# Seven half-size output products in the form with shared sums, one core of a Trainium2 chip

## The chip, the cores and the metric

The kernel runs on one core of a Trainium2 chip. A core has a matrix engine (TensorE, PE in the profile, with its weight loads listed apart as PEld), a vector engine (VectorE, DVE), a scalar engine (ScalarE, ACT), a general engine (GpSimd, POOL) and a queue engine that issues most transfers (SyncE, SP). Matmul results go to PSUM, which has eight banks of 512 fp32 columns by 128 partitions here. Each engine takes its instructions in order and waits on semaphores for the others. The metric is the device time of the program in microseconds (us); lower is better.

## What is computed

Linear attention without a mask over 8 batches, 8 heads, 576 positions and head size 64, followed by a two-layer network with an exact gelu. Cut to what matters:

```python
def _attn_ref(q, k, v):                      # 8 x 8 x 576 x 64
    q_s = softmax(q, axis=-1)
    k_s = softmax(k, axis=2)
    kv = np.einsum('bhsd,bhse->bhde', k_s, v)
    return np.einsum('bhsd,bhde->bhse', q_s, kv)

def _moe_ref(x, w_in, w_out):                # x: 4608 x 512
    h = x @ w_in                             # 512 x 2048
    g = 0.5 * h * (1.0 + erf(h / sqrt(2)))
    return g @ w_out                         # 2048 x 512
```

The attention's output, with heads side by side, is `x`; the output is 4608 x 512 in fp32. The tolerance lets the matmuls run in bf16.

## The kernel before

**Chunks.** The 4608 rows are worked in nine chunks of 512 rows (`M`): chunk c = 0 to 7 takes the first 512 rows of batch c, and chunk 8 the last 64 rows (`R`) of all eight batches. For a chunk: exp of q and k on ACT (`exp_q`, `exp_k`), the sums of q and its scaling (`q_sums`, `q_scale`), a transpose of q by DMA (`xbar_step`), the matmuls of k and v (`kv_step`), the attention's output `xT` (`x_all`), the first layer with gelu into `g` (2048 x 512, bf16), and the second layer into the output. The attention for the next chunks is put between the matmuls of the second layer. The order within every engine is the order in which the program is written (`manual_schedule`), so the text of the kernel is the order of all queues.

**First layer.** Chunks 0 and 1 use plain matmuls (`h_phase`, `h_pairs`). From chunk 2 on `h_waves` uses a scheme with seven products of half-size blocks instead of eight, in a form where products add up in PSUM: letters A, B, C name the banks in which they do, and `r` a copy in SBUF. Its last lines turn the last two groups of A and of B into `g` by gelu, then make sums of blocks of `g` on DVE (`s_parts`). `turn_roles` then renames the PSUM banks for the next chunk; the names `bb`, `ba`, `x0` to `x3`, `kv0`, `kv1` stand for the eight banks.

**Second layer.** `g` is cut into four blocks, halves of the 2048 features (`UP`, `DN`) by halves of the 512 rows (`LO`, `HI`); `w_out` likewise into four, features by halves of the 512 columns. Chunk 0 uses plain matmuls (`y_mm`); chunks 1 to 7 use `y_phase` and chunk 8 `y_last`. These use seven products of half-size blocks too. The operands of a product are listed in `y_operands`; sums of blocks of `w_out` are made once by `mix_wo` into `w16` and `w7` or in place, and sums of blocks of `g` by `s_parts` for each chunk into `s12`, `s5` or in place. A product is 16 matmuls of 256 columns (two groups of 128 rows by eight groups of features; 8 in `y_last`, which treats the two groups of rows after each other).

In `y_phase` before, five banks (`bd`, `be`, `bb`, `bx`, `ba`) take the products. The common part, product 4 minus product 5, is kept in SBUF in fp32 (`f`, which is the tile `zeros32`); ACT or DVE copies or adds each product into the output tiles `y_sb`, and POOL adds two of the four blocks to the block `c22` (L848 to L851). Two products add up in one bank only where a bank is begun anew. `f` is copied by DVE in chunk 1 (L823) and by ACT from chunk 2 on (L814).

In chunks 3 to 7 product 3 is itself computed by a seven-product scheme with quarter-size blocks (`class Two`): 28 matmuls of 128 columns (L753) in place of 16 of 256. For it POOL makes five sums of weights once (`weights`), DVE makes three kinds of sums of `g` for each half of the features in each chunk (`sums`: `rows`, `diag`, `cols`), ACT copies a snapshot of the partial result (`snap`, `two_d`), and POOL corrects it (`corner`, `corner2`) and adds it to two blocks (`spread`).

**Work between the products.** `y_phase` gets a dictionary of functions and calls `after(i)` behind named points; the loop at the end of the kernel fills it: exp of q and k two chunks ahead on ACT, sums of q on DVE, casts of v and scaling of q on POOL, the load of a later chunk on SP, and before the last product `next_x` (the next chunk's x, the transpose, k and v matmuls). In front of `y_phase(1)` the program issues `exp_q(2, parts=2)` and `exp_k(2)`.

## Time and profile before

| | |
|---|---|
| median of 3 runs | 255.81 us (255.73 to 255.81) |
| span of the profiled execution, first to last instruction | 253.9 us |
| granted TensorE clock | 0.997 |
| chunk 1's products begin (chain) | 58.5 us |
| chunk 2's products begin | 85.3 us |
| chunks 3 to 7: products begin | 111.1, 136.8, 162.4, 188.0, 213.0 us |
| chunk 8's products begin | 238.1 us |
| PE's last matmul ends | 250.3 us |
| DVE busy from 124.5 to 150.1 us (one chunk) | 24.4 of 25.6 us |
| DVE busy from 238.1 to 250.3 us | 9.1 of 12.2 us |

The median is the whole device time of the program; the span is that of one execution taken with the profiler, and 1.9 us of the median lie outside it. Line numbers (L799) are those of the kernel before. A line can be that of a helper: all additions made by `tt` have L444, so these are told apart by their tiles (`y_sb`, `two`, `two_d`, `r`, `qb`). PE's matmuls are pipelined: the timeline gives the time of issue and a modelled end, the chain the stretch for which a group holds the chain, which begins 0.17 us later.

### The profile page before, as it was taken

How to read it: one execution, taken by the hardware profiler on the slowest of the kernel's cores; microseconds unless marked ns; L12 is line 12 of the kernel's file. 1: busy time of each engine (PE TensorE's matmuls, PEld its weight loads, DVE VectorE, ACT ScalarE, POOL GpSimd, SP SyncE). 2: the span in 40 equal slices, each digit the busy share in tenths (PEclk: the TensorE clock that was granted, in tenths of full speed). 3: DMA queues.
4: the chain of work that ended last, by engine and by line, in shares of the span. 5: the costliest groups of instructions: out<-in, count | busy, mean ns of one | idle time of the engine just before them, and what ended most of it. 6: DMA issues, size and time to landing. Idle time of an engine off the chain costs nothing.

```text
span 253.9 us, 6825 instructions
## 1 busy us (share of the span) xinstructions
PE 247.9 (98%) x2738; PEld 196.1 (77%) x2738; DVE 219.1 (86%) x395; ACT 190.4 (75%) x326; POOL 102.8 (40%) x177
## 2 busy tenths in 40 slices
PE   7999999999999999999999999999999999999994
PEld 3444444448888888898889988998889889988883
DVE  1878898788987997998999899989999999868972
ACT  4785978699977996889688968896887788248711
POOL 1530023000978459106950596059603960560000
PEclk9999999999999999999999999999999999999998
DMA  7999999995329999890569255810520061004033
GB/s 239 397 367 420 405 406 400 401 407 206 61 64 288 375 265 377 246 340 5 188 196 310 98 188 177 204 36 3 165 87 3 1 193 57 3 4 165 0 84 84
DMA packets 43168, 50.24 MB, mean 198 GB/s; under 512 B 20225, under 2 KB 30465, under 8 KB 42881
## 3 DMA queue, kind: packets, MB, share of 16 engines
q1 hardware_dynamic: 42416, 49.13, 57.8%
q10 hardware_dynamic: 720, 0.69, 1.0%
q8 instruction: 21, 0.34, 0.6%
q14 instruction: 11, 0.08, 0.1%
HBM read 36.70 MB, written 9.44 MB: 182 GB/s over the span
## 4 chain that ended last, share of the span: by engine, by line
PE 81%; DMA 16%; DVE 1%; SPq 0%; issue 0%
PE qa L513 19%; PE ya L799 10%; PE qb L513 10%; PE yd L799 10%; DMA f<-in_q_dram 7%; PE ye L799 6%; PE ps L393 6%; PE yb L799 5%; PE qc L513 5%; DMA w<-in_moe_w_out_dram 3%; DMA w<-in_moe_w_in_dram 3%; PE yx L753 3%; DMA f<-in_v_dram 2%; PE kv L231 2%; PE ps L359 1%; PE ya L882 1%
## 5 line engine op out<-in xcount | busy, mean ns | idle before, releaser
L513 PEld LDWEIGHTS <-quad_s 128*128 128x128 bf16 x448 | 43.8, 98 | 5.1
L799 PEld LDWEIGHTS <-g 128*128 128x128 bf16 x368 | 35.2, 98 | 4.8 <-issue 0.4
L513 PEld LDWEIGHTS <-wi_bf 128*128 128x128 bf16 x336 | 32.8, 98 | 3.9
L799 PEld LDWEIGHTS <-s 128*128 128x128 bf16 x336 | 32.7, 98 | 3.7
L513 PE MATMUL qa<-quad_t,quad_s 128*128 128x256 bf16 x224 | 29.2, 273 | 0.0
L275 POOL TENSOR_TENSOR e<-e,recq 128x1024 bf16<-128x1024 bf16 (+1 forms) x4 | 9.3, 2330 | 47.8 <-DVE recq L270 41.0
L393 PE MATMUL ps<-xT,wi_bf 128*128 128x512 bf16 x128 | 28.1, 379 | 0.2 <-DVE kvc L244 0.2
L444 POOL TENSOR_TENSOR y_sb<-y_sb 128x128 f32<-128x128 f32 x56 | 26.0, 498 | 2.8 <-issue 2.8
L269 DVE TENSOR_REDUCE qsum<-e 128x16 f32<-128x1024 bf16 (+1 forms) x12 | 20.9, 1746 | 6.8 <-ACT e L179 6.5
L284 POOL TENSOR_TENSOR e<-e,recq 128x256 bf16<-128x256 bf16 x40 | 24.7, 653 | 1.8 <-DVE recq L270 1.2
L393 PEld LDWEIGHTS <-wi_bf 128*128 128x128 bf16 x128 | 12.4, 98 | 15.3 <-issue 0.7
L521 ACT COPY qc<-qa 128x512 f32<-128x512 f32 x26 | 13.9, 577 | 11.4 <-PE qa L513 5.3
L399 ACT ACTIVATE g<-ps 128x512 bf16<-128x512 f32 x32 | 17.6, 602 | 6.1 <-PE ps L393 5.8
L179 ACT ACTIVATE e<-f 128x512 bf16<-128x512 f32 (+1 forms) x42 | 20.5, 556 | 2.1 <-DMA f<-in_q_dram 1.9
L537 ACT ACTIVATE g<-r 128x512 bf16<-128x512 f32 x28 | 17.3, 631 | 6.3 <-DVE r L444 6.3
L444 DVE TENSOR_TENSOR qb<-qa,r 128x512 f32<-128x512 f32 x28 | 18.1, 691 | 4.1 <-PE qa L513 1.6
L537 ACT ACTIVATE g<-qc 128x512 bf16<-128x512 f32 x28 | 15.2, 594 | 7.4 <-PE qc L513 7.4
L418 DVE TENSOR_TENSOR s<-g 128x1024 bf16<-128x1024 bf16 x28 | 19.8, 726 | 0.0
L196 POOL CAST v_aug<-f 128x576 bf16<-128x576 f32 x25 | 17.0, 711 | 4.4 <-DMA f<-in_v_dram 4.3
L444 DVE TENSOR_TENSOR r<-qa,r 128x512 f32<-128x512 f32 x28 | 17.9, 680 | 0.7 <-PE qa L513 0.7
L184 ACT ACTIVATE ek<-f 128x2304 bf16<-128x2304 f32 (+1 forms) x10 | 17.2, 1734 | 1.2 <-DMA f<-in_k_dram 1.2
L1213 POOL CAST scr<-g 128x1 f32<-128x1 bf16 x4 | 0.7, 187 | 42.3 <-DVE g L421 42.3
(117 smaller groups left out, 550.2 us busy)
## 6 DMA issues: line engine op xcount, KB each, us to landing
out_dram<-y_sb SPq DMA_DIRECT2D x16, 512.0 KB, 3.9
f<-in_k_dram SPq DMA_DIRECT2D x6, 1152.0 KB, 9.5
f<-in_v_dram SPq DMA_DIRECT2D x6, 1152.0 KB, 10.5
f<-in_q_dram SPq DMA_DIRECT2D x6, 1024.0 KB, 7.6
w<-in_moe_w_in_dram SPq DMA_DIRECT2D x6, 512.0 KB, 8.9
f<-in_v_dram SPq DMA_DIRECT2D x8, 288.0 KB, 6.5
f<-in_q_dram SPq DMA_DIRECT2D x4, 512.0 KB, 9.0
w<-in_moe_w_out_dram SPq DMA_DIRECT2D x2, 1024.0 KB, 11.4
```

What stands on the lines that cost most here:

```text
L179: nc.scalar.activation(out=dst[:, i], in_=src[:, u], func=AF.Exp)
L184: nc.scalar.activation(out=ek[b % 2][:, i:i + n], in_=st[b]["kf"][:, i:i + n].rearrange("p x (n d) -> p x n d", n=NS), func=AF.Exp,)
L196: eng.tensor_copy(out=o, in_=i)
L269: nc.vector.reduce_sum(out=qsum, in_=st[b]["eq"][:, :, i * w:(i + 1) * w, :], axis=AX.X)
L284: nc.gpsimd.tensor_tensor(out=e, in0=e, op=ALU.mult, in1=st[b]["recq"][:, j, i:i + 4].unsqueeze(2).to_broadcast([128, 4, D]),)
L393: nc.tensor.matmul(ps, wi_bf[:, dm, t * 128:(t + 1) * 128], st[c]["xT"][:, dm, :], start=(dm == 0), stop=(dm == NDM - 1),)
L399: nc.scalar.activation(out=st[c]["g"][:, t, :], in_=ps, func=AF.Gelu)
L418: tt(out=s12[:, a, half], in0=g[:, a, half], in1=g[:, b, hi], op=ALU.add)
L444: eng.tensor_tensor(out=out, in0=in0, in1=in1, op=op)
L513: nc.tensor.matmul(held[kind, q][:, u], w, mov[m][:, k], start=(m in (1, 5) and u == 0 and k == 0), stop=(k == 1), skip_group_check=True,)
L537: nc.scalar.activation(out=g[:, t:t + 2, half], in_=held[kind, q], func=AF.Gelu)
L799: nc.tensor.matmul(ps[:, j * HN:(j + 1) * HN], act[m][:, k, j * 128:(j + 1) * 128], wgt[m][:, k, :], start=(first and k == 0 and j == 0), ...
```

## The change

The seven products of the second layer take another form of the scheme. With g's blocks a11 (`UP`, `LO`), a12 (`DN`, `LO`), a21 (`UP`, `HI`), a22 (`DN`, `HI`) and w_out's blocks b11, b12, b21, b22 there are four sums of each, each built on the one before:

- s1 = a21 + a22, s2 = s1 - a11, s3 = a11 - a21 (in place of a21), s4 = a12 - s2
- t3 = b22 - b12, t2 = t3 + b11, t4 = b21 - t2, t1 = b12 - b11 (in place of b12)
- products: 1: a11 b11, 2: a12 b21, 3: s4 b22, 4: a22 t4, 5: s1 t1, 6: s2 t2, 7: s3 t3

Product 1 is copied out by ACT (the first part of c11); products 6, 7 and 4 then add up on it in the same bank `pa`. Product 5 is copied out by DVE (into c22); after product 6 DVE writes pa + c22 into product 5's bank `pb`, and product 3 adds up there, which gives c12. Product 2 has a bank of its own, `pc`, and is added to c11 by DVE. After product 7 DVE adds pa to c22. After product 4 ACT copies pa out as c21. POOL does no addition of the output any more. The class `Two` and all that serves it are gone, for all chunks. `h_waves` puts gelu of the last two groups of B ahead of those of A, and the calls of `s_parts` are placed anew. The points of `after` and the functions at them change with the products.

```diff
     def s_parts(c, p0, n, which):
...
+        a11, a12, a21, a22 = g[:, a, lo], g[:, b, lo], g[:, a, hi], g[:, b, hi]
+        s1, s2, s4 = s5[:, a], s12[:, a, lo], s12[:, a, hi]
+        ops = {
+            1: (s1, a21, a22, ALU.add), 2: (s2, s1, a11, ALU.subtract),
+            3: (a21, a11, a21, ALU.subtract), 4: (s4, a12, s2, ALU.subtract),
+        }
+        for i in which:
+            tt(*ops[i])
...
+        gelu("B", 2, 3)
         gelu("A", 2, 3)
-        gelu("B", 2, 3)
-        if sums:
-            sums(c, 1)
-        else:
-            s_parts(c, 0, 4, (0,))
-            if mid:
-                s_parts(c, 0, 4, (4,))
-            s_parts(c, 0, 4, (2,))
-            s_parts(c, 4, 4, (0,))
-        s_parts(c, 4, 4, (3,))
-        s_parts(c, 4, 4, (4,))
+        s_parts(c, 0, 4, (2, 3, 4) if mid else (3, 4))
+        s_parts(c, 4, 4, (1, 2, 3, 4))
         turn_roles()
...
         wgt = {
+            1: wo_bf[:, UP, 0:HN], 2: wo_bf[:, DN, 0:HN], 3: wo_bf[:, DN, HN:DM],
+            4: w7, 5: wo_bf[:, UP, HN:DM], 6: w16[:, 1], 7: w16[:, 0],
         }
...
-    class Two:
...
+    def y_phase(c, ins):
...
+        at = {"ya": 2, "yb": 0, "yc": 3} if c == 1 else {"ya": roles["ba"], "yb": roles["bb"], "yc": roles["x0"]}
+        pa, pb, pc = (bank(at[n], n) for n in ("ya", "yb", "yc"))
...
+        mm(1, pa, True)
+        nc.scalar.copy(out=c11, in_=two(pa))
+        after(1)
+        mm(5, pb, True)
+        nc.vector.tensor_copy(out=c22, in_=two(pb))
+        after(5)
+        mm(6, pa, False)
+        tt(two(pb), two(pa), c22)
         after(6)
+        mm(2, pc, True)
+        tt(c11, c11, two(pc))
+        after(2)
+        mm(7, pa, False)
+        tt(c22, two(pa), c22)
         after(7)
+        mm(3, pb, False)
+        nc.scalar.copy(out=c12, in_=two(pb))
+        y_store(c, 0, ysb[0])
         after(3)
+        mm(4, pa, False)
+        nc.scalar.copy(out=c21, in_=two(pa))
         y_store(c, 1, ysb[1])
         after(4)
...
     def y_last(c):
...
+        sets = (("ba", "bb", "x0"), ("x2", "x1", "x3"))
...
         for j in range(2):
+            mm(j, 1, pa, True)
+            nc.scalar.copy(out=c11, in_=pa)
...
+            mm(j, 5, pb, True)
+            nc.scalar.copy(out=c22, in_=pb)
+            mm(j, 6, pa, False)
+            tt(pb, pa, c22)
+            mm(j, 2, pc, True)
+            tt(c11, c11, pc)
...
     y_phase(1, {
+        1: [sums[3], lambda: norm_q(2, 0, 2)],
+        5: [lambda: norm_q(2, 1, 2, nc.vector)],
+        6: [lambda: cast_v_all(3), lambda: xbar_step(2), lambda: exp_q(3)],
+        2: [lambda: kv_step(2), lambda: exp_k(3), lambda: q_sums(3)],
+        3: [lambda: table(AF.Gelu)],
         4: [lambda: load(4), lambda: x_all(2, (3, 4, 1, 5)),
...
     for c in range(2, B + 1):
...
         if nb <= B:
+            yi[1] = [lambda: exp_q(nb)]
+            yi[6] = [lambda: q_sums(nb), lambda: q_scale_parts(nb)]
+            yi[7] = [lambda: table(AF.Gelu)]
         if nb + 1 < B:
+            yi[6].append(lambda: load(nb + 1))
...
         if nb < B:
+            yi[5] = [lambda: exp_k(nb), touch_s, lambda: cast_v_all(nb)]
         if c < B:
+            yi[3] = [lambda: next_x(c, nb)]
+            y_phase(c, yi)
```

`touch_s` is a one-column copy on POOL from the last sum s4, which holds POOL's casts back until the sums are made; before, `touch_g` did so from `g`. `y_last` handles each of its two row groups in the same order of products; in the second one product 4 is made in two halves of 128 columns in two banks of their own, as product 7 was before.

## The prediction

> **What bounds the kernel now.** I read the page's shares first, then the chain of waits, then the timelines of ScalarE (ACT), VectorE (DVE) and TensorE (PE) around each place where the output products begin. From the page:

> ```profile
> PE 247.9 (98%) x2738; PEld 196.1 (77%) x2738; DVE 219.1 (86%) x395; ACT 190.4 (75%) x326; POOL 102.8 (40%) x177
> ...
> PE 81%; DMA 16%; DVE 1%; SPq 0%; issue 0%
> ```

> The chain is DMA until 41 us and then PE alone. It shows how evenly (start, length, what):

> ```profile
> 58.54 1.75 PE yd L799 x16
> 60.28 1.75 PE ye L799 x16
> ...
> 111.11 0.67 PE yx L753 x12
> ...
> 113.53 0.92 PE yx L753 x16
> ```

> From 44 to 250.3 us PE never pauses: each half-size product is 16 matmuls of 256 columns in 1.75 us (109 ns each), and the next begins where it ends. So an edit matters in two ways only: it changes what PE issues, or it makes PE wait. Work taken from DVE or POOL is worth nothing as long as PE does not wait for them now, and it does not.

> **The change, term by term.** All sums are in the profiled execution: span 253.9 us. The median of the runs is 255.81, so 1.9 us lie around the span, and I carry these over.

> *1. The inner scheme of product 3 (chunks 3 to 7).* Out go 12 + 16 matmuls of 128 columns, in come 16 of 256. The chain gives the 28 matmuls as 0.67 + 0.92 in three chunks and 0.67 + 0.97 in two, together 8.05 us; five times 1.75 is 8.75. PE: **+0.7** (bounds 0.55, all at 1.64, to 0.8, all at 1.59).

> *2. DVE and POOL.* Per chunk 3 to 7 DVE loses six small sums (0.41, 0.28, 0.41, twice: 2.2 us), two of ten wide sums (0.68 each) and one of five output operations (0.65): about 4.2 us. POOL loses the 56 adds of y_sb (26.0 us), the 30 on two_d and y_sb (16.1) and the weight sums (7.1). DVE's setup of w_out goes from ten operations of 0.69 to eight; DVE there waits 1.0 us for the load of w_out at 40.36, which hides either number. Each is **0**, since PE, which runs without a gap over all of them, is the cover; were it gone, DVE's 4.2 us a chunk would count.

> *3. New waits.* Before, five banks took the products and PE waited for no reader. Now products 6, 7 and 4 accumulate in the bank of product 1 and product 3 in that of product 5, so PE must wait until ACT has copied product 1 (before product 6), until DVE has read the bank after product 6 (before 7), and after 7 (before 4). The forms are all in the trace: ACT copies of 512 columns 0.57, DVE copies or adds from PSUM 0.63 to 0.69, also with PSUM as the output. I follow the waits chunk by chunk.

> *Chunk 1.* The copy of product 1 is on ACT; the first product's copy was on DVE (L823). ACT executes in order, and ahead of that copy it has exp of q and of k for chunk 2:

> ```profile
> 57.90 1.27 ACT L399 ACTIVATE g<-ps 128x512 bf16<-128x512 f32 x2
> 59.19 1.28 ACT L179 ACT_TABLE_LOAD   x1
> 60.48 2.38 ACT L179 ACTIVATE e<-f 128x512 bf16<-128x512 f32 x6
> 62.76 2.11 ACT L184 ACTIVATE ek<-f 128x2304 bf16<-128x2304 f32 x1
> 64.78 2.17 ACT L179 ACTIVATE e<-f 128x512 bf16<-128x512 f32 x4
> ```

> The copy takes the slot at 64.78, ends at 65.35, and product 6 can start at about 65.4. By PE's issue times, 0.17 ahead of the chain's, it was due at 61.87. PE waits **3.55 us**. Queued behind that copy on ACT are exp of q and k for chunk 3, each 0.5 us later, which DVE's sums of q need.

> Then PE: product 6 from 65.4, product 2 from 67.2, the k·v matmuls of chunk 2 at 69.0, product 7 at 69.8, product 3 at 71.5, product 4 due at 73.3. Behind the k·v matmuls DVE has four small operations (66.99 to 67.80 in the timeline), and then:

> ```profile
> 67.80 2.27 DVE L269 TENSOR_REDUCE qsum<-e 128x32 f32<-128x2048 bf16 x1
> 70.18 0.35 DVE L270 RECIPROCAL recq<-qsum 128x32 f32<-128x32 f32 x1
> 70.45 0.63 DVE L444 TENSOR_TENSOR y_sb<-y_sb,yb 128x512 f32<-128x512 f32 x1
> ```

> From k·v's end (69.9): 0.81 to the reduction, then 2.65 to the next add, now the one that reads the bank after product 7: 73.35 to 74.03. Product 4 starts at 74.1: **0.8 us** more. Chunk 1 costs 3.55 + 0.8 = **+4.35** (bounds 3.5, if the second wait is covered, to 4.6, with 0.2 for restarts; the trace's restart of PE behind DVE's kvc at 44.12 has 0.17 idle).

> *Chunk 2.* Product 5 is now second and needs sum 1 of all of g. DVE's second half of it stands fifth behind the r sums: from 84.36, the first taking 0.86, then 0.61 each, it runs 87.05 to 87.73. PE needs it at the fifth matmul of product 5, 85.14 + 1.75 + 0.44 = 87.33. With 0.1 for restart, 0.5; if the first takes 0.60, because POOL's tensor_scalar at its side (84.14 to 85.63) is gone, 0.25. I take **+0.4** (bounds 0 to 0.8).

> *Chunks 3 to 7.* In chunk 3, PE's last matmul of the first layer is issued at 110.95. ACT swaps its last two pairs of gelu, so those of half A run 111.88 to 112.96; the first frees product 5's bank at 112.5, due 112.70. Sum 1's second half starts at 112.03, when the B pair ends (DVE starts a wide sum there today, for the same reason), ends 112.71, needed 113.14. ACT's copy of product 1 ends 113.5, due 114.45. DVE after product 6: 116.4 to 117.1, due 117.94. The sums of q (2.65 us) hold the later adds to 119.75 to 120.95; the bank of product 2 is due at 121.4 for the next x, product 4 later still. All are covered, by 0.2 to 1 us: **0** (bounds 0 to 0.3 a chunk, 1.5 in all).

> *Last rows.* There a product lasts only 0.87 us, so the same gelu order is not covered (ACT, then PE):

> ```profile
> 236.76 1.23 ACT L537 ACTIVATE g<-r 128x512 bf16<-128x512 f32 x2 [0.56 <-DVE r L444]
> 237.89 1.07 ACT L537 ACTIVATE g<-qa 128x512 bf16<-128x512 f32 x2
> 238.85 1.09 ACT L537 ACTIVATE g<-qb 128x512 bf16<-128x512 f32 x2
> ```

> ```profile
> 237.91 1.04 PE L882 MATMUL yd<-wo_bf,g 128*128 128x256 bf16 x8
> 238.79 1.04 PE L882 MATMUL yx<-wo_bf,g 128*128 128x256 bf16 x8
> ```

> Product 5 is due at 238.79 and its bank is freed by the first gelu of the last pair, 239.45: **+0.7** (0.3 to 1.0). Later waits there fit by 0.1 to 0.2. The tail, two half products with an add and a store each, stays.

> *4. Queues.* SP's order becomes load, store, transpose, store; the transpose waits for POOL's scaling of q, until about 13.7 us after the products begin, and the store behind it frees a buffer that the next chunk needs 15 us later: **0**; without that cover a late store would delay ACT's or DVE's copy. The v load waits for POOL's casts, now done at about 6 us after the start instead of 10: **0**.

> **Sum:** 0.7 + 4.35 + 0.4 + 0 + 0.7 = 6.15 us; 255.81 + 6.15 = **262.0 us**.

> **Rivals.**
> *A. PE restarts slowly after chunk 1's pause.* At the kernel's start the weight loads show a slow phase:

> ```profile
> 5.87 0.34 PEld L1014 LDWEIGHTS ps<-zeros 128*128 128x128 f32 x1 [0.52 <-issue]
> 6.72 0.20 PEld L1014 LDWEIGHTS ps<-zeros 128*128 128x128 f32 x1 [0.52 <-issue]
> 7.16 0.19 PEld L1014 LDWEIGHTS ps<-zeros 128*128 128x128 f32 x1 [0.24 <-issue]
> ```

> Their spacing is 0.86 us until 6.72 and 0.43 after: half rate from 1.43 to 6.72, 5.3 us. If a 3.5 us pause brought that back, the same 5.3 us would hold 2.65 us less work: 264.65. Against it: no later pause in the trace is long enough to show it. [...]

> *B. The thin covers of chunks 3 to 7 fail too.* At 0.3 us each, +1.5: 263.5. For it: the cover of product 5's bank is 0.2 us; against: the timelines of those chunks repeat within 0.1 us.

> *C. Chunk 1's copy is covered.* That needs ACT to be free near 60.3, with exp of k done. Then 255.81 + 0.7 + 0.4 + 0.7 = 257.6. ACT's order is in the program, so little speaks for it.

> *D. Faster.* One mechanism: DVE and POOL traffic slows every matmul, and their relief lets it run. Place: the 1,560 full-size matmuls of chunks 2 to 8. Price: down to the weight load's mean of 98 ns, 11 ns each, -17 us: 245. It decides from 6.15 us / 1,560 = 4 ns each, below 105 ns. Against it: a matmul takes 109 ns in the last 12 us, where POOL is idle and DVE 74% busy, and also where DVE is 95% busy.

> **Chances.** Forecast 0.68, A 0.12, B 0.10, C 0.06, D 0.04. Adding the low bounds: 0.55 + 3.5 + 0 + 0.3 = 4.35, 260.2; the high ones without B: 0.8 + 4.6 + 0.8 + 1.0 = 7.2, 263.0. With A and B the range is 260.2 to 264.6. A measurement tells 0.2% (0.5 us) from no change; faster has D, 0.03, no change 0.01, slower 0.96.

> **What would show it.** A PE gap of 3.5 us at about 62 us, ended by ACT's copy of ya; a second, 0.8 us, before product 4, ended by DVE; 0.4 us within chunk 2's product 5; none of over 0.1 in chunks 3 to 7; 0.7 at the second product of the last rows; product 3 at 1.75 us everywhere. The prediction is wrong if ACT's copy comes before the exps, if PE's matmuls behind the first gap are not 109 ns apart, or if chunks 3 to 7 get longer by more than the 0.14 us of term 1.

## The result, and the profile after

| | before | after |
|---|---|---|
| median of the runs beside each other | 255.77 us (255.61 to 255.81) | 264.49 us (264.43 to 264.65, 4 runs) |
| ratio, 95% interval | | 1.0347 (1.0332 to 1.0361) |
| span of the profiled execution | 253.9 us | 262.4 us |
| granted TensorE clock in the mean | 0.997 | 0.993 |
| chunk 1's products begin (PE's issue) | 58.37 us | 58.10 us |
| chunk 2's first layer begins (PE's issue) | 72.81 us | 78.50 us |
| chunks 3 to 7: products begin (chain) | 111.1 to 213.0 us | 117.7 to 220.1 us |

The change makes the kernel slower by 8.7 us, where 6.15 were forecast. The page of the changed kernel, its shares and the chain's:

```profile
PE 251.1 (96%) x2678; PEld 196.9 (75%) x2678; DVE 190.0 (72%) x336; ACT 190.1 (72%) x324; POOL 54.5 (21%) x85
...
PEclk9999999999799999999999999999999999999999
...
PE 73%; DMA 12%; ACT 7%; DVE 4%; issue 1%; POOL 1%; ACTq 1%; SPq 0%; DVEq 0%
```

DVE gave up 29 us and POOL 48, and neither gave the program anything. ACT and DVE now hold 11% of the chain, where PE and DMA held 97% of it and DVE 1%. One slice of the clock row shows a 7: it covers 65.6 to 72.2 us. There stands chunk 1, here in PE's timeline of the changed kernel (time of issue, length, what; in brackets the idle time before and what ended it):

```profile
58.10 2.01 PE L684 MATMUL ya<-wo_bf,g 128*128 128x256 bf16 x16
59.95 1.91 PE L684 MATMUL yb<-wo_bf,s 128*128 128x256 bf16 x16
65.12 3.50 PE L684 MATMUL ya<-w,s 128*128 128x256 bf16 x16 [3.26 <-ACT y_sb L695]
68.41 2.03 PE L684 MATMUL yc<-wo_bf,g 128*128 128x256 bf16 x16
...
75.39 1.91 PE L684 MATMUL ya<-w,g 128*128 128x256 bf16 x16 [0.59 <-DVE y_sb L430]
```

Product 6 was due at 61.70 (59.95 + 1.75) and is issued at 65.12; then its 16 matmuls take 3.50 us where a product elsewhere shows 1.91. From issue to issue that is 3.29 us, 206 ns a matmul. The engines that PE waits for, in their timelines of the changed kernel, first ACT, then DVE:

```profile
60.21 2.37 ACT L173 ACTIVATE e<-f 128x512 bf16<-128x512 f32 x6
62.49 2.11 ACT L178 ACTIVATE ek<-f 128x2304 bf16<-128x2304 f32 x1
64.50 0.56 ACT L695 COPY y_sb<-ya 128x512 f32<-128x512 f32 x1
```

```profile
72.06 2.27 DVE L263 TENSOR_REDUCE qsum<-e 128x32 f32<-128x2048 bf16 x1
74.44 0.35 DVE L264 RECIPROCAL recq<-qsum 128x32 f32<-128x32 f32 x1
74.71 0.63 DVE L430 TENSOR_TENSOR y_sb<-ya,y_sb 128x512 f32<-128x512 f32 x1
```

The copy of product 1 stands behind exp of q and k, and the add after product 7 behind the sums of q, both as forecast. All waits of PE for another engine (total, times, longest, in us); those for `scr` and `kvc` lie in the kernel's opening, as in the kernel before, where they have 1.4 and 0.3 too:

```profile
PE ya L684 <- ACT y_sb L695: 3.3, 1, 3.3
PE ps L862 <- DVE scr L90: 1.4, 1, 1.4
PE ya L684 <- ACT g L522: 0.8, 1, 0.8
PE ya L684 <- DVE y_sb L430: 0.6, 1, 0.6
PE yb L737 <- ACT g L522: 0.6, 1, 0.6
PE ps L353 <- DVE kvc L238: 0.3, 1, 0.3
```

The third is in chunk 2, the fifth in the last rows. Their timeline lines, PE and the gelu ahead of it on ACT, then PE in the last rows:

```profile
90.62 1.07 ACT L522 ACTIVATE g<-qb 128x512 bf16<-128x512 f32 x2
91.58 1.09 ACT L522 ACTIVATE g<-qa 128x512 bf16<-128x512 f32 x2
```

```profile
91.74 1.91 PE L684 MATMUL ya<-wo_bf,g 128*128 128x256 bf16 x16 [0.83 <-ACT g L522]
...
246.79 1.03 PE L737 MATMUL yb<-wo_bf,s 128*128 128x256 bf16 x8 [0.55 <-ACT g L522]
```

Where the span's +8.5 us stand, each from the two timelines or chains: start of chunk 1's products -0.27 (why was not followed); pause before product 6 +3.42; half clock in products 6 and 2 +1.66 (3.29 us from issue to issue against 1.75, and 1.96 against 1.84); product 4's wait +0.75; chunk 2 +0.9; chunks 3 to 7 +0.7; last rows +0.7; from PE's last matmul to the end +0.5. The terms add up to 8.4; the rest is 0.1 in chunk 1's first product. Another 0.2 us of the median lie outside the span.

### The profile page after: what moved, and what is told of

Same layout as the page of the kernel before. It is cut to its first block, busy times and chain, and to the rows that moved or that the text cites. A ratio compares the mean times of both kernels' runs of the same rounds, so it can differ in the third digit from the quotient of the medians.

```text
span 262.4 us, 6525 instructions
## 1 busy us (share of the span) xinstructions
PE 251.1 (96%) x2678; PEld 196.9 (75%) x2678; DVE 190.0 (72%) x336; ACT 190.1 (72%) x324; POOL 54.5 (21%) x85
## 4 chain that ended last, share of the span: by engine, by line
PE 73%; DMA 12%; ACT 7%; DVE 4%; issue 1%; POOL 1%; ACTq 1%; SPq 0%; DVEq 0%
PE ya L684 18%; PE qa L498 16%; PE yb L684 8%; PE qb L498 8%; DMA w<-in_moe_w_in_dram 6%; PE ps L387 5%; PE yc L684 5%; PE qc L498 4%; DMA f<-in_v_dram 4%; ACT g L522 3%; PE ya L737 2%; DMA touch<-in_moe_w_out_dram 2%; PE kv L225 2%; PE ps L353 2%; PE yb L737 1%
## 5 line engine op out<-in xcount | busy, mean ns | idle before, releaser
L684 PEld LDWEIGHTS <-g 128*128 128x128 bf16 x448 | 43.3, 98 | 7.9 <-issue 2.2
L684 PEld LDWEIGHTS <-s 128*128 128x128 bf16 x336 | 33.6, 100 | 7.9 <-issue 3.4
L684 PE MATMUL ya<-w,g 128*128 128x256 bf16 x224 | 26.8, 273 | 0.6 <-DVE y_sb L430 0.6
L684 PE MATMUL yb<-wo_bf,s 128*128 128x256 bf16 x224 | 26.7, 273 | 0.0
L710 ACT COPY y_sb<-yb 128x512 f32<-128x512 f32 x7 | 4.1, 587 | 21.4 <-PE yb L684 21.4
L269 POOL TENSOR_TENSOR e<-e,recq 128x1024 bf16<-128x1024 bf16 (+1 forms) x4 | 9.3, 2332 | 48.8 <-DVE recq L264 48.8
L378 DVE CAST xT<-ps 128x512 bf16<-128x512 f32 x18 | 11.7, 687 | 10.0 <-PE ps L353 8.4
L684 PE MATMUL ya<-w,s 128*128 128x256 bf16 x112 | 15.0, 292 | 3.3 <-ACT y_sb L695 3.3
```

The costliest lines, as they stand in the source:

```text
L269: eng.tensor_tensor(out=e, in0=e, in1=st[b]["recq"].unsqueeze(3).to_broadcast([128, J, w, D]), op=ALU.mult,)
L378: nc.vector.tensor_copy(out=st[b]["xT"][:, hp, :], in_=ps)
L684: nc.tensor.matmul(ps[:, j * HN:(j + 1) * HN], act[m][:, k, j * 128:(j + 1) * 128], wgt[m][:, k, :], start=(first and k == 0 and j == 0), ...
```

## The experiments

Three questions were open: what the half clock costs and what brings it on (it was a rival of 0.12 and came in all four runs), whether the other terms are what the timelines say, and whether the new form is worth anything once its waits are gone.

### The clock behind the pause: filling it

In the first three kernels PE multiplies into an unused bank ahead of product 6 in chunk 1, 30, 12 and 4 times; the result is not used.

```diff
         after(5)
+        if c == 1:
+            fill = bank(4, "fill")
+            for i in range(30):
+                nc.tensor.matmul(fill[:, 0:HN], act[1][:, i % HK, 0:128], wgt[1][:, i % HK, :],
+                                 start=True, stop=True, skip_group_check=True)
         mm(6, pa, False)
```

> Thirty extra matmuls of 256 columns into a spare bank (109 ns each, 3.3 us) fill chunk 1's pause before product 6; nothing waits for them. If PE's idleness is what makes product 6 slow (3.50 us for 16 matmuls, granted clock 0.52), product 6 takes 1.75 us again, the pause itself stays in the form of extra matmuls, and the time is 264.5 - 1.7 = 262.8 us. If product 6 is slow for another reason (its operands, its bank, POOL or DVE at its side), it stays at 3.5 us and the time at 264.5.

Measured: 262.63 us (262.42 to 262.93), ratio 1.0275 (1.026 to 1.0291), granted clock 1.0 in every run. In PE's timeline of this kernel product 6 is back at its length, though it starts as long behind its due time as before (64.87 against 61.45, 3.42 us):

```profile
61.45 3.44 PE L703 MATMUL fill<-wo_bf,g 128*128 128x256 bf16 x30
64.87 1.91 PE L684 MATMUL ya<-w,s 128*128 128x256 bf16 x16
```

So the half clock comes from PE's idleness and not from the new form of accumulation. It is worth 264.49 - 262.63 = 1.9 us, or 1.6 if each is set against the kernel before that ran beside it (255.77 and 255.53). The next two leave 1.95 and 2.82 us of the pause idle:

> Twelve extra matmuls in front of the same pause: PE is idle for about 1.95 us instead of 3.26. If the clock falls only after a pause of nearly 3.3 us, 262.8 us; if any pause of 2 us does it, 264.5; if the fall depends on how the pause lies against a window that runs freely, runs of both kinds.

> Four extra matmuls: PE is idle for about 2.8 us. 262.8 us if the clock stays up, 264.5 if it falls; both in different runs if a free window decides.

Measured: with 12 matmuls 262.55, 262.57, 264.58 and 264.71 us, clocks 1.0, 1.0, 0.993 and 0.99; with 4 matmuls 262.51 to 262.86 (ratio 1.0275, 1.026 to 1.029), clock 1.0 in every run. The longer idle time let the clock fall in no run, the shorter in two of four: length alone does not decide. (Runs without a trace are counted as falls by a granted clock of 0.994 or less, with which the longer times come.) Both and the changed kernel itself were run again at another time:

> The changed kernel once more, for the number of its runs in which the clock falls behind the pause of 3.3 us: in the 16 runs with this pause so far 12 had a granted clock of 0.994 or less and 1.7 to 2 us more. If the pause is just at the edge of a window that runs freely, runs of both kinds again, near 262.5 and 264.5; if the changed kernel always falls, 264.5 in all six.

> The pause cut to 1.95 us, again: two of four runs fell. By a window that has to be idle as a whole (3.4 us) none should fall; by a window of which about half has to be idle, about half of the runs.

> The pause cut to 2.8 us, again: none of four runs fell, though two of four did with 1.95 us. If length decides, at least as many fall here as with 1.95 us; none again would mean that the place of the pause in time matters more than its length.

Measured: the changed kernel 264.06 us, ratio 1.0318 (1.0296 to 1.034), at clock 0.993 in three of five runs and 1.0 in the two others (263.31, 262.68); 12 matmuls 263.54 us, three of six at 0.990 to 0.993 (264.39 to 264.7), the rest at 262.57 to 262.68; 4 matmuls 264.31 us, now all four at 0.990 to 0.993. What looked like "2.82 us never falls" was wrong.

### A theory that fits: a grid of 3.41 us windows

The traces then gave another reading. At the kernel's start the spacing of the weight loads goes from 0.86 to 0.43 us. Here are the loads of the changed kernel (columns as in the timelines above):

```profile
5.88 0.34 PEld L862 LDWEIGHTS ps<-zeros 128*128 128x128 f32 x1 [0.52 <-issue]
6.73 0.34 PEld L862 LDWEIGHTS ps<-zeros 128*128 128x128 f32 x1 [0.52 <-issue]
7.40 0.19 PEld L862 LDWEIGHTS ps<-zeros 128*128 128x128 f32 x1 [0.33 <-issue]
7.83 0.19 PEld L862 LDWEIGHTS ps<-zeros 128*128 128x128 f32 x1 [0.24 <-issue]
```

The interval of 0.67 us from 6.73 to 7.40 is part slow, part full: x / 0.86 + (0.67 - x) / 0.43 = 1 gives x = 0.48, so the clock rose at 7.21. (The granted-clock column of the profile reads 1.00 there all the same, so this phase rests on the spacing alone.) The same sum gives 4.77 in e12_fill4_again. In stretches of 0.05 us the granted clock of the changed kernel has a mean of 0.73 in 65.20 to 65.25 and of 0.64 in 68.60 to 68.65, so the half clock stands from 65.22 to 68.64, 3.41 us. From 7.21 to its start it is 58.01 us, 17 times 3.412. The same sums, with the granted clock in stretches of 0.4 us, give 58.04 us, 17 times 3.414, in e5_swap (7.26 to 65.30) and 61.43 us, 18 times 3.413, in e12_fill4_again (4.77 to 66.20); there too the half clock lasts 3.41 to 3.42 us. So from the traces a window is put at 3.413 us, the mean of the three. Counting such windows from 7.21, the seventeenth ends at 65.23. The table of stretches on that grid, for the changed kernel (stretch; length; busy us and instructions of PE, weight loads, DVE, ACT, POOL; granted clock; DMA share; GB/s):

```profile
58.41:61.82 3.41, 3.41 (x31) 2.77 (x30) 1.93 (x6) 3.38 (x6) 0.00 (x0) 1.00 0.49 195
61.82:65.24 3.42, 0.16 (x3) 0.11 (x2) 3.32 (x6) 3.42 (x6) 2.07 (x2) 1.00 0.00 0
65.24:68.65 3.41, 3.41 (x18) 2.35 (x17) 0.97 (x1) 3.41 (x5) 3.32 (x4) 0.50 0.35 81
68.65:72.06 3.41, 3.41 (x97) 2.92 (x96) 2.13 (x6) 0.52 (x1) 0.00 (x0) 1.00 0.33 73
```

The clock is 0.50 in one window, from edge to edge, behind the window in which PE was busy for 0.16 us. In e12_fill4_again, with a grid that lies elsewhere (4.77 + 18 x 3.413 = 66.20), the half clock sits in the window that begins there, though PE had already worked for 1.26 us:

```profile
62.80:66.21 3.41, 1.26 (x12) 1.13 (x12) 3.17 (x5) 3.41 (x5) 3.21 (x2) 1.00 0.00 0
66.21:69.62 3.41, 3.41 (x18) 2.44 (x17) 0.70 (x1) 2.80 (x3) 2.18 (x4) 0.50 0.68 154
```

And in the profiled run of e10_after_again, which is the changed kernel, the same pause is cut by an edge of the grid, and the clock stays:

```profile
60.57:63.99 3.42, 1.57 (x15) 1.26 (x13) 2.46 (x5) 3.42 (x7) 0.54 (x1) 1.00 0.06 20
63.99:67.40 3.41, 1.99 (x19) 1.78 (x19) 2.43 (x3) 3.41 (x7) 3.41 (x3) 1.00 0.00 0
```

The traces up to here: a fall behind windows with 0.16 (twice: this kernel and e5_swap), and 1.26 us busy; none where the least busy window had 1.45 (e6_last), 1.46 (e2_fill12), 1.57, 1.67 or 2.44. The window of e2_fill12, which holds its whole pause:

```profile
63.04:66.45 3.41, 1.46 (x15) 1.30 (x14) 2.98 (x4) 3.41 (x6) 3.41 (x2) 1.00 0.00 0
```

So the theory, an estimate from these traces: the phase of the grid against the kernel's start differs from run to run (PE's first work is at about 1.45 us in each trace, the rise at 4.6 us in e1_fill30 and at 7.6 in e14_long), and the clock halves for the next window if PE was busy for less than some 1.26 us (e12_fill4_again, which fell) to 1.45 us (e6_last, which did not) of 3.41, that is, idle for about 1.96 to 2.15. Four runs test it. In one, 17 filling matmuls leave 1.4 us idle; in another exp of k is issued twice, which lengthens the pause to 5.4 us; two are fresh traces.

```diff
     exp_k(2)
+    exp_k(2)
```

> 17 matmuls of 256 columns fill the head of chunk 1's pause and leave about 1.4 us of it idle. Theory G (the clock is decided on a grid of windows of 3.41 us that starts at PE's first rise to the full clock, and halves behind a window in which PE was busy for less than about 1.35 us, so idle for more than about 2.0): 1.4 us idle can fill no window to that point, no run falls, all at the level without a fall, 262.5 to 262.9 us, granted clock 0.995 or more in each. Rival H (any pause of more than about 1 us lets the clock fall in about half of the runs, whatever its length): three of six runs near 264.5, clock 0.99.

> exp of k for chunk 2 is issued twice, so ACT's copy of product 1 comes 2.1 us later and the pause is 5.4 us; the output is the same. Theory G: of two neighbouring windows one is always idle for over 2.0 us, so every run falls: 262.7 + 2.1 + a half-rate phase that is worth 0.7 to 2.1, 265.5 to 266.9, no run under 265.3. Rival H (a fall in some 6 or 7 of 10 runs at any length): one to three of six runs at 264.8, the others at 266.7.

> The changed kernel once more, for one more trace. Theory G: count windows of 3.413 us from the time at which the spacing of the first weight loads goes from 0.86 to 0.43 us. If PE is busy for less than 1.26 us in a window at 58 to 69 us, the granted clock is 0.50 through the whole next window and at no other time; if it is busy for more than 1.45 in each, it stays 1.00; between the two, open. Rival H: the start and end of a half-rate phase lie off that grid.

> The kernel with 12 filling matmuls once more, 1.95 us idle, for one more trace. Theory G: the least busy window holds 1.46 us, at the edge between the falls and the stays seen so far (1.26 and 1.45); if it falls, the half-rate phase fills the next window of the grid exactly, and the fall needs a window that holds the whole pause. If the pause is cut by a grid line, so that each part is under 1.9 us, no fall. Rival H: a fall also where a grid line cuts the pause.

Measured: e13_fill17 262.75 us (262.5 to 262.96, 5 runs), ratio 1.0273 (1.0259 to 1.0287), clock 0.998 or more in each. e14_long 267.09 us (266.58 to 267.29, 4 runs), ratio 1.0442 (1.0426 to 1.0458), clock 0.983 to 0.987 in each. e15_after_third 262.93 us at clock 1.0 with 1.78 us busy in its least busy window; e16_fill12_third 262.63 us with 2.19. So none of the short pause and all of the long one, and both fresh traces as the theory says, though neither fell and neither was near the edge (in both a grid line cut the pause). One thing went beyond it: the median of e14_long is 0.2 us above the upper bound that was given. Its stretches on the grid show why:

```profile
62.19:65.61 3.42, 0.00 (x0) 0.00 (x0) 3.32 (x6) 3.39 (x4) 2.46 (x2) 1.00 0.00 0
65.61:69.02 3.41, 1.76 (x9) 1.23 (x9) 0.58 (x1) 3.41 (x6) 2.93 (x4) 0.50 0.50 114
69.02:72.43 3.41, 3.41 (x18) 2.35 (x17) 0.70 (x1) 2.29 (x2) 0.00 (x0) 0.50 0.18 40
72.43:75.85 3.42, 3.42 (x97) 2.93 (x96) 2.24 (x6) 0.00 (x0) 0.00 (x0) 1.00 0.02 5
```

PE restarts at 67.26 in a half-rate window; 1.76 us of busy time at half rate were not enough to raise the clock at its end, so the next window is slow as well, and 5.17 us of work at half rate cost half of that, 2.6. All runs together, by idle time of the pause:

| idle in the pause | kernels | runs with the fall |
|---|---|---|
| 5.4 us | e14_long | 4 of 4 |
| 3.26 us | the changed kernel, e5_swap, e6_last, e10_after_again, e15_after_third | 15 of 22 |
| 2.82 us | e3_fill4, e12_fill4_again | 4 of 8 |
| 1.95 us | e2_fill12, e11_fill12_again, e16_fill12_third | 5 of 11 |
| 1.4 us | e13_fill17 | 0 of 5 |
| none | e1_fill30 | 0 of 4 |

For a pause L and a window W = 3.41, a window idle for t = 2.0 to 2.15 or more exists in a share (L + W - 2t) / W of all phases: 0.70 to 0.78 for 3.26 us, 0.57 to 0.65 for 2.82. The counts, 0.68 and 0.50, are near, which says little as long as runs made together are not independent (0 of 4, then 4 of 4 of one kernel). That would follow if such runs start in nearly the same phase; this was not tried.

The theory does not cover the falls at 1.95 us. Such a pause leaves at least 3.41 - 1.95 = 1.46 us busy in any window, and with 1.45 and 1.46 the clock stayed in e6_last and e2_fill12, yet five of eleven runs fell. No trace of such a fall is at hand. So the grid and the part that idle time plays are shown; the exact threshold, and what the chip counts, stay open.

### The waits, one by one

In e4_dvecopy DVE copies product 1 in chunk 1, in place of ACT:

```diff
-        nc.scalar.copy(out=c11, in_=two(pa))
+        (nc.vector.tensor_copy if c == 1 else nc.scalar.copy)(out=c11, in_=two(pa))
```

> Chunk 1's copy of product 1 goes to DVE instead of ACT, so that it stands behind no exp. My theory: the pause of 3.4 us and the slow clock (1.7 us) both go; product 7 then waits 0.85 us for DVE's add into product 5's bank (behind the sums and scaling of q) and product 4 1.2 us for DVE's second add, the latter 0.45 more than now; the next x starts 3.8 us sooner and the time is 260.7 us. If the pause were due to exp of k itself (something else that product 6 needs from ACT), the time would stay near 264.5.

Measured: 260.77 us (260.55 to 260.91), ratio 1.0201 (1.0184 to 1.0218), 0.1 from the number expected. PE's timeline of this kernel:

```profile
61.57 1.91 PE L684 MATMUL ya<-w,s 128*128 128x256 bf16 x16
...
66.95 1.91 PE L684 MATMUL ya<-w,g 128*128 128x256 bf16 x16 [0.96 <-DVE yb L430]
...
71.53 1.91 PE L684 MATMUL ya<-w,g 128*128 128x256 bf16 x16 [0.93 <-DVE y_sb L430]
```

Product 6 no longer waits. DVE, with one more operation, holds up product 7 by 1.0 us (66.95 against 65.93), which did not wait before, and product 4 by 1.1 in place of 0.75. Chunk 2's first layer begins 3.85 us earlier than in the changed kernel, of which the half clock is 1.7. Moving the copy took away a pause of 3.42 us and brought 1.4 us of other waits, on DVE's adds, which end at 66.89 after product 6 and at 71.48 after product 7.

In e5_swap two banks change roles behind the first layer of chunk 2, so that product 1's bank is one that gelu frees earlier:

```diff
         turn_roles()
+        if c == 2:
+            roles["ba"], roles["x2"] = roles["x2"], roles["ba"]
```

> The changed kernel with two bank names exchanged after chunk 2's first layer, so that product 1 takes the bank of the second group of A (read long before) and not that of the last group of B. My theory: product 1 of chunk 2 waited 0.83 us for its bank; it now starts at once, and product 5 waits about 0.35 us inside for the second half of sum 1: 264.5 - 0.5 = 264.0 us, with the pause of chunk 1 untouched (slow clock or not as its runs fall). Rival: product 1 waited for the gelu of its operand, and the 0.8 us stay.

Measured: 263.81 us, median of six, five of them with the fall. In PE's timeline of this kernel:

```profile
90.78 1.91 PE L686 MATMUL ya<-wo_bf,g 128*128 128x256 bf16 x16
92.53 2.23 PE L686 MATMUL yb<-wo_bf,s 128*128 128x256 bf16 x16
94.60 1.91 PE L686 MATMUL ya<-w,s 128*128 128x256 bf16 x16
```

Product 1 has no idle time before it and starts 0.96 us earlier than in the changed kernel. So the wait was for the bank and not for the operand. Product 5 then lasts 0.32 longer: that is the wait for the second half of sum 1 (in the chain there DVE's sums stand from 91.93 to 93.23, and product 5's last twelve matmuls follow from 93.28), which the forecast had and the larger wait for the bank had hidden. Product 6 gains 95.23 - 94.60 = 0.6.

In e6_last product 1 of the second group of rows is issued before product 5 of the first, and the second group's stores of c22, which stand ahead of ACT's copy of c12, go by SP alone:

```diff
-            mm(j, 1, pa, True)
+            if j == 0:
+                mm(0, 1, pa, True)
+                mm(1, 1, banks[1][0], True)
...
-            store(1, j, HN, both if j else (sp, sp))
+            store(1, j, HN, (sp, sp))
```

> The changed kernel with two edits in the last rows: product 1 of the second row group is issued behind that of the first (0.87 us of PE work in front of product 5), and one store of the second group goes to SP alone, so that ACT's copy of c12 stands behind no store. My theory: product 5's wait of 0.7 us for its bank is covered, and the stretch from PE's end to the kernel's end goes from 4.06 back to about 3.5 us; together 264.5 - 1.2 = 263.3 us. Rival for the end: the last store itself takes longer, and the 4.06 us stay: 263.8.

Measured: 262.85 us, median of six, three with the fall (263.53 to 264.03; the others 261.8 to 262.17). The wait of 0.6 for gelu is gone. The tail isn't mended: 4.1 us from PE's end to the end of the span, as in the changed kernel (before: 3.6), though ACT's copy of c12 now follows product 3 at once (its end 255.16, the copy 255.19). The runs with the fall lie at the rival's 263.8. The stores of c22 were issued on SP, behind others, instead of on ACT.

### The inner scheme, and the form without waits

In e7_plain3, the kernel before computes product 3 in chunks 3 to 7 as a plain product:

```diff
-        p3 = y3 if 2 < c < B else None
+        p3 = None
```

> The kernel before with product 3 plain in chunks 3 to 7, and nothing else changed: no sums for the inner scheme on DVE, no correction on POOL. If PE alone counts, +0.7 us on the kernel before (255.5 to 256.2). If the relief of DVE (2.2 us a chunk) and POOL were worth anything, less than that, down to 255.5 or below.

Measured: 256.78 us (256.5 to 256.89), ratio 1.004 (1.0028 to 1.0053), so 0.7 to 1.35 us, with the median above the number expected; the chain grows by 0.10 to 0.16 us in each of the five chunks, 0.7 in all, and the rest was not found. From chunk 3 to chunk 4 it is 25.80 us in this kernel and in the changed one alike, 25.64 in the kernel before. Here is the chain of e7_plain3, then that of the changed kernel:

```profile
110.94 1.75 PE yd L799 x16
112.68 1.75 PE yx L799 x16
...
136.74 1.75 PE yd L799 x16
```

```profile
117.71 1.75 PE ya L684 x16
119.45 1.75 PE yb L684 x16
...
143.51 1.75 PE ya L684 x16
```

The last two kernels keep the new form and take all its waits away: DVE copies product 1 in chunk 1, the roles are swapped in chunk 2, product 1 of the second row group comes early, sums of q and the scaling move behind later products in chunk 1, and the sums of g have another order. In e9_fixed2 that order holds in chunk 2 only, DVE copies the second group's c12, and the stores go to both queues as in the changed kernel.

```diff
-        nc.scalar.copy(out=c11, in_=two(pa))
+        (nc.vector.tensor_copy if c == 1 else nc.scalar.copy)(out=c11, in_=two(pa))
...
+        if c == 2:
+            roles["ba"], roles["x2"] = roles["x2"], roles["ba"]
...
-        2: [lambda: kv_step(2), lambda: exp_k(3), lambda: q_sums(3)],
+        2: [lambda: kv_step(2), lambda: exp_k(3)],
+        7: [lambda: q_sums(3)],
```

> The changed kernel with all waits that the trace shows taken away: chunk 1's copy of product 1 on DVE, there the scaling of q behind DVE's add into product 5's bank and the sums of q for chunk 3 behind the add after product 7; chunk 2's banks exchanged and sum 1 of the second half ahead of sums 3 and 4; both edits in the last rows. If the form itself (accumulating in one bank, DVE writing PSUM) costs nothing and all the loss was these waits and product 3, 255.5 + 0.7 = 256.2 us. If there is a cost of the form that I have not seen, 257 us or more.

> The kernel with all waits taken away, with two edits of its own mended: sums 3 and 4 of the first half stand ahead of the second half's sums again except in chunk 2 (putting them behind made product 7 of the last rows wait 0.8 us), and in the last rows DVE copies c12 and the stores go to both queues again. 258.4 - 0.8 - 0.5 = 257.1 us if PE's end and the queues of the last stores are what is left above the kernel before; about 256.5 if the end goes back to 3.5 us behind PE's end. At 257.8 or more there is another cost.

Measured: e8_fixed 258.4 us (257.79 to 258.45), ratio 1.0099 (1.0084 to 1.0114), 2.2 above the number expected: no output product waits in chunks 1 to 7, but the new order of the sums made product 7 wait 0.8 us in the last rows, and the tail with the second group's stores of c22 on SP took 4.2. e9_fixed2 256.88 us (256.67 to 257.42), ratio 1.0052 (1.0039 to 1.0064), between the two numbers expected, span 254.8: 0.9 above the span before. PE ends 0.64 later (250.97 against 250.33; term 1 is 0.7 of it, another 0.3 and an earlier start of 0.35 nearly cancel), and the tail is 0.26 longer (3.83 against 3.57). So the form itself costs the plain product 3 and little else, its waits and the clock behind them cost all the rest, and even without them the relief of DVE and POOL buys nothing. No kernel here beats the one before.

## Why the prediction was right or wrong

The direction and most of the waits held. What failed is the step that let PE run at the full clock again right behind chunk 1's pause; with it the forecast was 2.6 us short. The time, 264.49 us, lies at the very top of the range (260.2 to 264.6), which only rival A's price reaches; as the ratio of 1.0347 on the forecast's 255.81 it is 264.7, just above. One of the prediction's own signs of being wrong came: the matmuls behind the first gap are 206 ns apart, not 109. Point by point, by the prediction's own steps:

- *Term 1, the inner scheme:* +0.7 forecast, 0.7 measured in the changed kernel and alone in e7_plain3.
- *Term 2, DVE and POOL:* 0 forecast, and 0 shown: e9_fixed2 has DVE busy for 75% of the span instead of 86% and is no faster. Rival D falls with it: a product lasts 1.75 us in chunks 3 to 7, to the hundredth as before.
- *Chunk 1's pause:* 3.55 forecast, 3.42 measured, ended by ACT's copy behind exp of k; e4_dvecopy removes it. Rival C falls, and its price with it: even with the copy off ACT's queue the time is 260.77 and not 257.6, since DVE's adds then come late.
- *Product 4:* 0.8 forecast, 0.75 measured, by DVE's sums of q.
- *Rival A, the step that failed.* The prediction gave it 0.12, an estimate: the trace of the kernel before has no pause that could have shown it. The half clock came in 15 of 22 runs with this pause; it cost 1.66 us in the trace, and 1.2 to 2.1 between runs of one kernel with and without it. A window need not lie wholly in the pause: one that was 37% busy (1.26 of 3.41 us, e12_fill4_again) was enough. With that, a pause of 3.26 us hits in 0.70 to 0.78 of all phases, so by what the runs show A was the likeliest case. A's price of 2.65 was too high: it was taken from the start's 5.3 us of half rate, of which the windows show 3.41 us here, so 1.7, near the 1.66 of the trace.
- *Chunk 2:* +0.4 for sum 1 forecast, 0.9 measured, from another place. In this chunk the last group of B stands in the bank that `turn_roles` hands to product 1, so product 1 itself waits until ACT's gelu has read it at 91.7. The prediction followed the sums on DVE and product 5's bank, and never asked which instruction last reads product 1's bank in this chunk. That this term was of the right order is luck. The wait that it forecast is real, 0.3 us, and appears when the other is gone (e5_swap).
- *Chunks 3 to 7:* 0 forecast and none there, so rival B falls: covers of 0.2 us held.
- *Last rows:* +0.7 forecast, 0.7 measured. "The tail stays" was wrong: +0.5. In the timeline of the changed kernel the store at 257.06 keeps ACT's queue for 0.96 us, and the copy of c12 behind it follows at 258.06:

```profile
257.06 0.96 ACTq L728 DMA_DIRECT2D out_dram<-y_sb  x1
...
258.06 0.37 ACT L764 COPY y_sb<-yb 128x256 f32<-128x256 f32 x1 [0.64 <-PE yd L737]
258.46 1.43 ACTq L728 DMA_DIRECT2D out_dram<-y_sb  x2
```

  That this order makes the tail longer is only a reading of the trace, and e6_last speaks against it: there the store of c22 is off ACT's queue, the copy comes at once, and the tail is no shorter. e9_fixed2 moved the copy to DVE and got 0.24 us of the 0.5 back. The cause of the longer tail stays open.
- *Term 4, queues:* 0 forecast; no wait of PE points to one, except for that tail.

The sum with the measured terms: 0.7 + 3.42 + 0.75 + 0.9 + 0.7 = 6.5 us of span without the clock, against 6.15 forecast; then 1.66 for the clock, 0.5 for the tail, 0.2 outside the span and -0.27 at the start give 8.6 of the 8.7.

## What to carry to other kernels

Where an accumulation takes over a bank, list for every chunk, the odd ones too, which instruction on which engine reads that bank last and what stands ahead of it in its queue; each of the four new waits is of that kind. Price a pause of the matrix engine of about 2 us or more with the half clock that may follow, as a chance that grew with its length here (none of 5 runs fell at 1.4 us, 5 of 11 at 1.95, 4 of 8 at 2.82, 15 of 22 at 3.26, 4 of 4 at 5.4), and compare runs of such a kernel by their granted clock before reading anything into 2 us. Work taken from an engine for which nobody waits was worth nothing here, be it 29 or 48 us.
